# Batch 0's spectra made twice for one filter tile, tables issued by SP, and another order of the first loads

## The chip, the core and the metric

The kernel runs on one core of a Trainium2 chip. The metric is device time in microseconds of one execution. The kernel before took 525.09 us in the median of three runs (524.14 to 527.62). A core has five engines with a queue of instructions each: PE (TensorE, matrix products into PSUM), DVE (VectorE), ACT (ScalarE), POOL (GpSimd) and SP (SyncE, which only issues transfers here). POOL's transfers can turn float32 into float16 on the way; SP's only copy. Engines run side by side and wait for one another through semaphores.

## The reference

```python
def _attn_ref(x, filt_r, filt_i):             # x: 8 x 3136 x 256
    X = np.fft.rfft(x, axis=1)
    F = (filt_r + 1j * filt_i)[None, :, :]    # 1569 x 256
    return np.fft.irfft(X * F, n=x.shape[1], axis=1)

def _moe_ref(x, U, V, w_ch1, w_ch2):          # x: the result above
    xt = x.transpose(0, 2, 1)
    h = xt @ U @ V                            # rank 32, over the sequence
    u = x + h.transpose(0, 2, 1)
    ch = np.maximum(u @ w_ch1, 0.0) @ w_ch2   # 256 -> 1024 -> 256
    return u + ch
```

So each of 8 batches goes through a Fourier transform over 3136 positions, a product with a filter of one complex number per frequency and channel, the transform back, a low-rank mixing over the sequence, and a two-layer perceptron per position.

## The kernel before

**The transform.** 3136 is 64 x 49. A first matmul (with `w64`, 64 points) gives 32 slots `s`, each a complex part; a second one per slot (table `t2`, 98 x 128) does the 49 points and leaves, for one slot, the real parts of its spectrum on partitions 0 to 63 and the imaginary parts on 64 to 127. The product with the filter follows on DVE, then a matmul per slot with the inverse table (`g12`) and a last matmul with `s2`. The kernel calls the steps f1, forward, product, inverse. Slots are worked in 16 pairs `m`; tables and filters are cut in four `PARTS` of eight slots.

**The filter product.** `ft` has two halves in its columns: filt_r and filt_i. The first half is copied to partitions 64 to 127 (`swap_real`, L221), the second is copied there with its sign turned (`swap_imag`, L228). `both_products` (L521) reads one PSUM bank `px` twice, once against each half, in one DVE instruction of 1024 elements. The matching inverse table has two halves as well: `g`, and `g` with its upper and lower 64 rows exchanged. The second half of part 0 is loaded ready-made (`gs`, L247); those of parts 1 to 3 are made by two POOL copies each (`swap_table`, L186). Batches 0 and 1 use this form. From batch 2 on `product` (L531) uses three DVE instructions and a POOL addition.

**Batch 0** does not go through DRAM. `first_f1` (L356) makes the 64-point transform in groups of four rows for half the channels (`dh`), evicted by ACT and DVE in turn into `at`. `first_a` (L385) turns two slots into the layout of forward, evicted by ACT into `a`. `first_mid` (L399) then runs over m: the product of m on DVE, the inverse of m-1 on PE with two ACT evictions (`back`, L405), forward of m+2 (`ahead`, L421), `first_a` of m+3. Between sets of four pairs it makes the two filter copies of the next part. `keep_on` and `keep_in` (L342, L350) are matmuls whose result nobody reads. `fill` are 13 units of batch 1's f1 (`f1_units`, L457), four of them inside `first_mid`'s loop, four among its last transpositions, and the rest until the first perceptron group. At the end, seven groups of transpositions are evicted to `e2`, from which the low-rank part and the perceptron start.

**Batches 1 to 7** store f1's result to DRAM (`c1`, by SP for batch 1) and load it back as `a` (`load_a`, L493, on SP), likewise after the inverse (`c2`, `load_e`). Their steps are laid out by hand on `slots`: 48 slots per batch, two for every two hidden blocks of a group of four row pairs. `put(slot, gen)` names the slot at which a step's instructions are written into all queues; each engine then works its queue strictly in the written order. mm1 (L707), mm2 (L722) and the stores of `out` fill the slots themselves.

**The loads** stand at the start of POOL's queue, in this order: x of batch 0 in three chunks, called x(0,0), x(0,1), x(0,2) here, with single filter rows (`load_rest`) after the first and x's odd last row after the last; filters of part 0, tables `t2` and `g` of part 0, `gs`; then for each further part table t2, filters, table g, with the copies of `swap_table` a part later; x(1,0), U, x(1,1), x(1,2), V (`vq`), four pieces of `w1`, `w2` (as `w2n`), x(2,0); then 14 copies that reorder V (`v_order`, L277), x(2,1), and two copies that reorder w2. POOL lets eight transfers be under way: a ninth waits for the first.

**PSUM** has eight banks: tags x and f one each, m four, o two.

Of the kernel before, what the change touches and what calls it, by code (L numbers as in the profile page):

```python
# [26 lines left out]
def _consts():  # L27
# [22 lines left out]
    for s in range(NS):  # L50
        for j in range(49):
# [10 lines left out]
            if s:  # L62
                t2[s, :49, j], t2[s, 49:, j] = e.real, -e.imag
                t2[s, :49, 64 + j], t2[s, 49:, 64 + j] = sg * e.imag, sg * e.real
                g[s, j] = np.concatenate([ei.real, ei.imag]) * 2
                g[s, 64 + j] = np.concatenate([-ei.imag, ei.real]) * 2 * sg
            else:
                o = 0 if j < 25 else 49
                t2[s, o:o + 49, j] = e.real
                t2[s, o:o + 49, 64 + j] = e.imag  # L70
                g[s, j, o:o + 49] = ei.real * (2 if f else 1)
                g[s, 64 + j, o:o + 49] = -ei.imag * 2

    t2[0, :, 64] = 0
    t2[0, 49:, 64] = (-1.0) ** r
    g[0, 64] = 0
    g[0, 64, 49:] = (-1.0) ** r
    g *= ESC / n
    gs = np.concatenate([g[:, 64:], g[:, :64]], 1)
# [5 lines left out]
            np.ascontiguousarray(g.reshape(4, 8, 128, 98).transpose(0, 2, 1, 3)).astype(f16),  # L85
            np.ascontiguousarray(gs[0:8].transpose(1, 0, 2)).astype(f16))
# [3 lines left out]
def kernel(  # L90
# [13 lines left out]
    w64_np, s2_np, idn_np, fold_np, wp_np, t2_np, g_np, gs_np = _consts()  # L104
# [7 lines left out]
    gs_d = nc.inline_tensor(gs_np, name="gsd")  # L112
# [8 lines left out]
    BUFS = {"x": 1, "f": 1, "m": 4, "o": 2}  # L121

    def bank(tag, name):
        return ps.tile([128, 512], F32, tag=tag, bufs=BUFS[tag], name=name)

# [21 lines left out]
    def load_x(b, c, parts=None):  # L147
# [3 lines left out]
        for lo, hi in parts or ((c0[c], c0[c + 1]),):  # L151
            for h in range(2):
# [6 lines left out]
            if hi == NH:  # L159
# [3 lines left out]
                nc.gpsimd.dma_start(t[0:64, o:o + DM], rows(x, b, NR - 1, 1))  # L163
# [9 lines left out]
    nyq = sb.tile([128, DM], F32, tag="ocho", bufs=1, name="nyq")  # L173
    PARTS = ((0, 8), (8, 16), (16, 24), (24, 32))
    for a, b in PARTS:
        for c in (0, NS * DM):
            nc.vector.memset(ft[32:64, c + a * DM:c + b * DM], 0.0)  # L177

    def load_table(k, a, b):

        dst, src, w = ((t2, t2_d, 128), (g12, g_d, 98))[k]
        n, p = (b - a) * w, dst.shape[0]
        nc.gpsimd.dma_start(dst[:, a * w:b * w],
                            bass.AP(tensor=src, offset=a // 8 * p * n, ap=[[n, p], [1, n]]))

    def swap_table(a, b):  # L186

        o = NS * 98
        for p, q in ((0, 64), (64, 0)):
            nc.gpsimd.tensor_copy(g12[p:p + 64, o + a * 98:o + b * 98],  # L190
                                  g12[q:q + 64, a * 98:b * 98])

    def load_filters(a, b):

        d = max(a, 1)
        for c, src in ((0, filt_r), (NS * DM, filt_i)):
            nc.gpsimd.dma_start(
                ft[0:24, c + a * DM:c + b * DM],
                bass.AP(tensor=src.tensor, offset=a * DM, ap=[[64 * DM, 24], [1, (b - a) * DM]]))
            nc.gpsimd.dma_start(  # L200
                ft[25:49, c + d * DM:c + b * DM].rearrange("p (k d) -> p k d", d=DM),
# [3 lines left out]
    def load_rest():  # L205

        for c, src in ((0, filt_r), (NS * DM, filt_i)):
            nc.gpsimd.dma_start(
                ft[25:49, c:c + DM],
                bass.AP(tensor=src.tensor, offset=32 * DM, ap=[[64 * DM, 24], [1, DM]]))  # L210
            nc.gpsimd.dma_start(
                ft[24:25, c:c + NS * DM],
                bass.AP(tensor=src.tensor, offset=24 * 64 * DM,
                        ap=[[NS * DM, 1], [1, NS * DM]]))
        nc.sync.dma_start(
            nyq[64:65, :],
            bass.AP(tensor=filt_r.tensor, offset=(SEQ // 2) * DM, ap=[[DM, 1], [1, DM]]))

    def swap_real(a, b):

        nc.vector.tensor_copy(ft[64:128, a * DM:b * DM], ft[0:64, a * DM:b * DM])  # L221

    def swap_imag(a, b):

        fb = NS * DM
        if a == 0:
            nc.vector.memset(ft[0:1, fb:fb + DM], 0.0)
        nc.vector.tensor_scalar_mul(ft[64:128, fb + a * DM:fb + b * DM],  # L228
                                    ft[0:64, fb + a * DM:fb + b * DM], -1.0)
# [3 lines left out]
    for c in range(1, len(CH)):  # L233
        load_x(0, c)
# [4 lines left out]
    for k, part in enumerate(PARTS):  # L239
        if k:  # L240
            load_table(0, *part)
        load_filters(*part)
        if k == 0:
            load_table(0, *part)
        load_table(1, *part)
        if k == 0:
            nc.gpsimd.dma_start(g12[:, NS * 98:(NS + 8) * 98], gs_d.ap())  # L247
        if k > 1:
            swap_table(*PARTS[k - 1])
    load_x(1, 0)  # L250
    uq = sb.tile([128, NR * RANK], F16, tag="esb", bufs=2, name="uq")
    nc.vector.memset(uq[64:128, :], 0.0)
    nc.gpsimd.dma_start(uq[0:64, :], moe_U.rearrange("(q r) p -> q (r p)", q=NQ))
    load_x(1, 1)
    swap_table(*PARTS[3])
    load_x(1, 2)
    vqs = []
    for k in range(2):
        v = sb.tile([128, SEQ // 2], F16, tag="xt", bufs=5, name="vq")
        vqs.append(v)  # L260
        nc.gpsimd.dma_start(v[64:96, :], moe_V[:, k * (SEQ // 2):(k + 1) * (SEQ // 2)])
    w1 = cst.tile([128, 2 * 1024], F16)
    for i in range(4):
        nc.gpsimd.dma_start(
            w1[32 * i:32 * i + 32, :].rearrange("p (h c) -> p h c", h=2),
            bass.AP(tensor=moe_w_ch1.tensor, offset=moe_w_ch1.offset + i * 64 * 1024,
                    ap=[[1024, 32], [32 * 1024, 2], [1, 1024]]))
    w2 = cst.tile([128, 8 * DM], F16)
    w2n = sb.tile([128, 8 * DM], F16, tag="esb", bufs=2, name="w2n")
    nc.gpsimd.dma_start(w2n, moe_w_ch2.rearrange("(cc t) e -> cc (t e)", t=8))  # L270
# [6 lines left out]
    def v_order():  # L277

        for r in range(0, NR, 8):
# [8 lines left out]
            yield  # L288

# [60 lines left out]
    def keep_in(tile, n):  # L350

        for _ in range(n):
            nc.tensor.matmul(tile[:, 0:128], w64[:, :], idn[:, :],
                             start=True, stop=True, skip_group_check=True)

    def first_f1():  # L356
        ne = 0
        xs = [st[0]["x"][c] for c in range(len(CH))]
        for r0 in range(0, NH - 1, 4):
            for dh in range(2):  # L360
                keep_on(4 if r0 < 16 else 0)
# [6 lines left out]
                for h in range(2):  # L368
                    dst = atv[:, dh, :, h * NH + r0:h * NH + r0 + 4]
                    src = pa.rearrange("p (r h k) -> p h k r", h=2, k=64)[:, h]  # L370
                    if ne % 2:
                        nc.vector.tensor_copy(dst, src)
                    else:
                        nc.scalar.copy(dst, src)
                    ne += 1
        pa = bank("m", "pa")
        o = (NH - 1 - c0[-2]) * DM
        for dh in range(2):
            nc.tensor.matmul(pa[:, dh * 64:(dh + 1) * 64],
                             xs[-1][0:64, o + dh * 128:o + (dh + 1) * 128], w64[0:64, 0:64],  # L380
                             start=True, stop=True, skip_group_check=True)
        nc.scalar.copy(atv[:, :, :, NH - 1],
                       pa[:, 0:128].rearrange("p (e k) -> p e k", e=2))
# [13 lines left out]


    def first_mid(fill):  # L399
# [21 lines left out]
        def ahead(m, keep=0):  # L421
            return forward(m, st[0]["a"][m // 4], ("m",), keep)

        pxs = [ahead(0), ahead(1)]
        keep_on(8)
        for m in range(NS // 2):
            for k, part in enumerate(PARTS):
                if k and 2 * m == part[0]:
                    swap_real(*part)
                    swap_imag(*part)  # L430
# [509 lines left out]
```

## Time and profile before

| what | value |
|---|---|
| runs of before, median of 3 | 525.09 us (524.14 to 527.62) |
| the profiled execution: its time | 523.76 us |
| its span, first to last instruction | 522.0 us |
| DVE busy, ACT busy, POOL busy, of the span | 78%, 72%, 58% |
| first product of batch 0 starts | 19.98 us |
| first matmul of the perceptron (phh, L712) starts | 53.61 us |
| first forward of batch 1 (px, L516) starts | 64.45 us |
| HBM read, written | 56.25 MB, 48.17 MB |

All times in what follows are microseconds from the start of the span. "Busy" adds up the instructions of an engine. A row of the order in time gives start, length, engine, line, operation, result<-operands, and in brackets how long the engine had been idle and what ended that. A matmul's row includes the time until its result is in PSUM, so rows of PE overlap; the pitch from one start to the next is what a matmul costs in a series. Transfers issued by POOL have their landing on record, those issued by SP have not.

### The profile page before, as it was taken

To read this page: it belongs to the slowest core of one execution; us is meant where nothing else is said; L and a number is where in the kernel's file an instruction comes from. 1 tells how busy PE (TensorE), PEld (TensorE's weight loads), DVE (VectorE), ACT (ScalarE), POOL (GpSimd) and SP (SyncE) were. 2 spreads that over 40 slices of the span, in tenths; PEclk is the share of its full clock that TensorE was granted. 3 is DMA by queue.
4 is the path that set the end of the run, shared out by engine and by line. 5 is a ranking of instruction groups with operands and counts; after the bars stand their busy time and mean duration, and the time that the engine had idled before them with its cause. 6 is when DMAs were issued, how large, how long until landed. Compare 5 with 4: busy or idle time off the path is not lost.

```text
span 522.0 us, 11372 instructions
## 1 busy us (share of the span) xinstructions
PE 496.7 (95%) x3976; PEld 327.4 (63%) x3976; DVE 407.7 (78%) x585; ACT 377.5 (72%) x772; POOL 301.9 (58%) x430
## 2 busy tenths in 40 slices
PE   4878899999989999999999999999999999999997
PEld 3766477777656665666666666666666666555555
DVE  7897386677888888998998888988999877436654
ACT  2767757768778768887788878888777678665552
POOL 7798733445765757775777675965666564313001
PEclk9999999999999999999999999999999999999999
DMA  8989998978899798887898698888777575644325
GB/s 135 188 143 221 233 214 203 213 209 191 197 202 253 180 203 181 215 219 176 235 216 221 162 253 207 184 227 194 180 194 150 129 167 134 139 100 80 71 62 121
DMA packets 122571, 93.99 MB, mean 180 GB/s; under 512 B 58017, under 2 KB 104866, under 8 KB 122514
## 3 DMA queue, kind: packets, MB, share of 16 engines
q1 hardware_dynamic: 98986, 50.93, 39.1%
q0 software_dynamic: 20240, 40.60, 37.9%
q10 hardware_dynamic: 3288, 1.74, 1.3%
q8 instruction: 31, 0.51, 0.4%
q14 instruction: 26, 0.21, 0.1%
HBM read 56.25 MB, written 48.17 MB: 200 GB/s over the span
## 4 chain that ended last, share of the span: by engine, by line
PE 78%; DVE 9%; DMA 6%; POOL 3%; issue 2%; ACT 1%; ACTq 0%; SPq 0%; DVEq 0%; POOLq 0%
PE phh L712 28%; PE po L789 25%; PE px L516 5%; PE pi L552 5%; PE pu L637 4%; PE po L738 4%; DVE uv L537 4%; DMA xt<-in_x_dram 3%; PE pf L472 3%; PE ph L594 2%; DVE ft L177 1%; DVE uv L535 1%; DMA out_dram<-och 1%; DMA g<-gd 1%; DMA a<-c 1%
## 5 line engine op out<-in xcount | busy, mean ns | idle before, releaser
L720 ACT ACTIVATE h<-phh 128x512 f16<-128x512 f32 (+1 forms) x391 | 205.4, 578 | 68.6 <-PE phh L712 64.1
L712 PE MATMUL phh<-ut,w 128*128 128x512 f16 x768 | 197.5, 379 | 0.3 <-ACT h L720 0.3
L540 POOL TENSOR_TENSOR y<-uv 128x512 f16<-128x512 f16 x96 | 111.8, 1165 | 100.1 <-DVE uv L537 80.3
L789 PE MATMUL po<-h,w 128*128 128x512 f16 x656 | 168.5, 379 | 0.0
L712 PEld LDWEIGHTS <-w 128*128 128x128 f16 x832 | 114.2, 144 | 54.5 <-issue 0.9
L537 DVE TENSOR_TENSOR uv<-px,ft 64x512 f16<-64x512 f32 x192 | 132.1, 688 | 2.6
L807 POOL DMA_DIRECT2D out_dram<-och x148 | 85.9, 588 | 81.6 <-DVE och L799 38.9
L789 PEld LDWEIGHTS <-w 128*128 128x128 f16 x656 | 60.5, 98 | 57.8 <-issue 1.1
L535 DVE TENSOR_TENSOR uv<-px,ft 128x512 f16<-128x512 f32 x96 | 64.9, 676 | 35.2 <-PE px L516 33.0
L556 ACT CAST esb<-pi 98x512 f16<-98x512 f32 x112 | 65.9, 589 | 32.1 <-PE pi L552 28.2
L798 DVE TENSOR_TENSOR tt<-po,ut 128x512 f32<-128x512 f32 x82 | 56.7, 692 | 34.3 <-PE po L789 32.3
L799 DVE STREAM_TRANSPOSE och<-tt 128x512 f32<-128x512 f32 x82 | 58.4, 712 | 2.8
L516 PE MATMUL px<-a,t 98*128 98x256 f16 x256 | 49.1, 273 | 5.6 <-DVE uv L537 2.8
L478 ACT CAST asb<-pf 128x512 f16<-128x512 f32 (+1 forms) x80 | 46.1, 576 | 6.5 <-PE pf L472 3.8
L524 DVE TENSOR_TENSOR uv<-px,ft 128x1024 f16<-128x1024 f32 x32 | 38.0, 1219 | 11.7 <-PE px L516 11.2
L702 ACT CAST ut<-pu 128x512 f16<-128x512 f32 x82 | 44.8, 612 | 0.0
L516 PEld LDWEIGHTS <-t 98*128 98x128 f16 x256 | 22.7, 98 | 31.6 <-DVE uv L537 10.6
L552 PE MATMUL pi<-y,g 128*98 128x256 f16 x192 | 36.7, 272 | 0.1
L472 PE MATMUL pf<-xt,w 128*128 128x512 f16 (+1 forms) x91 | 33.2, 370 | 1.0 <-DMA xt<-in_x_dram 1.0
L738 PE MATMUL po<-w,h 128*128 128x256 f16 x256 | 33.2, 273 | 0.0
L552 PEld LDWEIGHTS <-g 128*98 128x98 f16 x256 | 29.6, 123 | 3.2 <-issue 0.8
L637 PEld LDWEIGHTS <-e 96*128 96x128 f16 x686 | 26.4, 98 | 7.2
(99 smaller groups left out, 420.0 us busy)
## 6 DMA issues: line engine op xcount, KB each, us to landing
xt<-in_x_dram POOLq DMA_DIRECT2D x46, 256.0 KB, 6.6
out_dram<-och SPq DMA_DIRECT2D x180, 64.0 KB
a<-c SPq DMA_DIRECT2D x28, 384.0 KB
e<-c SPq DMA_DIRECT2D x56, 192.0 KB
out_dram<-och POOLq DMA_DIRECT2D x148, 64.0 KB, 3.5
c<-esb SPq DMA_DIRECT2D x24, 384.0 KB
c<-asb POOLq DMA_DIRECT2D x30, 256.0 KB, 5.6
out_dram<-och POOLq DMA_DIRECT2D x12, 256.0 KB, 4.8
```

The costliest lines, as they stand in the source:

```text
L516: nc.tensor.matmul(px[:, sl * DM:(sl + 1) * DM], t2[:, s * 128:(s + 1) * 128], a2[:, (2 * ml + sl) * DM:(2 * ml + sl + 1) * DM], start=Tru ...
L535: nc.vector.tensor_mul(uv[:, 0:512], px[:, :], ft[:, a:a + 512])
L537: nc.vector.tensor_mul(uv[p:p + 64, 512:1024], px[q:q + 64, :], ft[q:q + 64, b:b + 512])
L540: nc.gpsimd.tensor_add(y, uv[:, 0:512], uv[:, 512:1024])
L552: nc.tensor.matmul(pi[0:98, sl * DM:(sl + 1) * DM], g12[:, g:g + 98], y[:, o:o + DM], start=(fi == 0), stop=(fi == nf - 1), skip_group_che ...
L556: nc.scalar.copy(split(esb[:, ml * 512:(ml + 1) * 512]), natural(pi[0:98, :]))
L712: nc.tensor.matmul(pm[:, 0:w], w1[:, dh * 1024:(dh + 1) * 1024].rearrange("p (c t) -> p t c", t=8)[:, t], ut[:, dh * w:(dh + 1) * w], star ...
L720: nc.scalar.activation(h[:, 0:w], pm[:, 0:w], RELU)
L789: nc.tensor.matmul(po[:, :], w2[:, t * DM + dh * 128:t * DM + (dh + 1) * 128], hs[gx, t][:, :], start=(t == 0), stop=(t == 7))
L798: nc.vector.tensor_add(tt, po[:, :], uts[gx][:, dh * 512:(dh + 1) * 512])
L799: nc.vector.transpose(och.rearrange("p (j h a) -> p h j a", h=2, a=32)[:, dh], tt.rearrange("p (j t) -> p j t", t=32))
L807: (nc.gpsimd if k and (b < nb - 1 or r0 > 12) else nc.sync).dma_start(dst, och[32 * i:32 * i + 32, k * 512:(k + 1) * 512] .rearrange("p (r ...
```

## The change

1. **One filter tile for batch 0.** filt_r is loaded to partitions 0 to 63 of `ft`, filt_i to 64 to 127. `ahead` makes a slot's real parts on both partition halves of one PSUM bank and its imaginary parts on both halves of a second one: eight matmuls with 64 columns of `t2` each, in pairs at column positions 0 and 64, instead of two with 128 columns. One DVE instruction multiplies both banks by the same 512 columns of `ft`. The copies between the sets of four are gone; the last frequency (f = 1568) becomes a row of its own in the tables, so the separate row `nyq` goes as well. `ft` is brought into the old form for the later batches by 16 DVE instructions (`spread_filters`), one at the end of `first_mid`, one after `make_u(0)`, 14 at slots 0, 1, 2, 3, 4, 5, 6, 8, 12, 17, 27, 30, 36, 44. Four of these turn a sign after batch 1.
2. **No negated table loaded.** `gs` goes. For each of the four parts POOL makes one copy (`swap_table`) and ACT one with the sign turned (`negate_table`, at m = 0, 4, 8, 12).
3. **Tables by SP.** `t2` and `g` are issued by SP. Ahead of each part stands a transfer of one element (`mark`) that reads an eviction of batch 0: that of row 12 in `first_f1` for part 0, that of `a`'s first piece of set 0, 1, 2 for parts 1, 2, 3; so SP holds the tables until then.
4. **POOL's order.** x's odd row stands ahead of x(0,2); filters of parts 0 and 1 follow, then swap 0, filters of parts 2 and 3, swap 1, U, x(1,0), swap 2, x(1,1), swap 3, x(1,2), V, w1, x(2,0), w2, eight of the 14 V copies, x(2,1), the w2 copies, the other six.
5. **PSUM** tag m lives in a pool of its own that is opened three times: for `first_f1`, for the two-bank `px` of `first_mid` (two buffers, so `ahead` of m+2 waits for the product of m), and for the rest.
6. **first_f1 and fillers.** ACT evicts one half of the channels, DVE the other. Fillers are laid out as 18, 4, 8, 4, 40, 3, 3, 3, 22, 0, 0, 0 between the groups; those inside `first_mid` go. One unit of `fill` stays in `first_mid`'s loop (m = 15), two follow it, five stand among the transpositions.
7. **Stores.** In batch 1, the first of eight stores of `out` goes from SP to POOL in five groups.

```diff
-            for c in (0, NS * DM):
-                nc.vector.memset(ft[32:64, c + a * DM:c + b * DM], 0.0)
+    for p in (32, 96):
+        nc.vector.memset(ft[p:p + 32, a * DM:b * DM], 0.0)
...
+    def spread_filters():
+        for a, b in PARTS:
+            lo, hi = slice(a * DM, b * DM), slice((NS + a) * DM, (NS + b) * DM)
+            for dst, src in ((ft[0:64, hi], ft[64:128, lo]), (ft[64:128, hi], ft[64:128, lo]),
+                             (ft[64:128, lo], ft[0:64, lo])):
+                nc.vector.tensor_copy(dst, src)
+                yield
+        for a, b in PARTS:
+            neg = ft[64:128, (NS + a) * DM:(NS + b) * DM]
+            nc.vector.tensor_scalar_mul(neg, neg, -1.0)
+            yield
...
+    def tables_behind(k, ap):
+        nc.sync.dma_start(mark[:, k:k + 1], ap)
+        for t in range(2):
+            load_table(t, *PARTS[k], eng=nc.sync)
...
+            if r0 == 12:
+                tables_behind(0, atv[0:1, 0, 0, r0:r0 + 1])
...
+        if ml == 0 and gi < 3:
+            tables_behind(gi + 1, st[0]["a"][gi][0:1, 0:1])
+            loads(gi + 1)
+            if gi == 2:
+                load_weights()
...
-        def ahead(m, keep=0):
-            return forward(m, st[0]["a"][m // 4], ("m",), keep)
+        def ahead(m):
+            px = pm[-1].tile([128, 1024], F32, tag="px", bufs=2, name="px")
+            for fi in range(2):
+                for sl in range(2):
+                    s, o = 2 * m + sl, fi * 512 + sl * DM
+                    for q in (0, 64):
+                        nc.tensor.matmul(
+                            px[q:q + 64, o:o + DM], t2[:, s * 128 + fi * 64:s * 128 + fi * 64 + 64],
+                            st[0]["a"][m // 4][:, s % KG * DM:(s % KG + 1) * DM],
+                            start=True, stop=True, tile_position=(0, q), skip_group_check=True)
+            return px
...
-            for k, part in enumerate(PARTS):
-                if k and 2 * m == part[0]:
-                    swap_real(*part)
-                    swap_imag(*part)
-            uv = both_products(m, pxs.pop(0))
+                nc.vector.tensor_mul(
+                    uv.rearrange("p (f e) -> p f e", f=2),
+                    pxs.pop(0).rearrange("p (f e) -> p f e", f=2),
+                    bass.AP(tensor=fap.tensor, offset=fap.offset, ap=[fap.ap[0], [0, 2], [1, 512]]))
...
+                if m % 4 == 0:
+                    negate_table(*PARTS[m // 4])
...
-                (nc.gpsimd if k and (b < nb - 1 or r0 > 12) else nc.sync).dma_start(
+                (nc.gpsimd if k and (b < nb - 1 or r0 > 12) or b == 1 and n == 0 and r0 < 20 else nc.sync).dma_start(
...
+    for t in (0, 1, 2, 3, 4, 5, 6, 8, 12, 17, 27, 30, 36, 44):
+        put(t, spread)
```

## The prediction

> **What bounds the kernel now.** I read the page first (who is busy), then a table of stretches, then the order in time of each engine over the first 65 us, which hold nearly all of the diff. Page, busy time:
>
> ```profile
> PE 496.7 (95%) x3976; PEld 327.4 (63%) x3976; DVE 407.7 (78%) x585; ACT 377.5 (72%) x772; POOL 301.9 (58%) x430
> ```
>
> Table of stretches (columns: stretch, its length, then PE, PEld, DVE, ACT, POOL busy, granted clock, DMA share, GB/s):
>
> ```profile
> 18.00:44.20 26.20, 21.81 (x328) 18.77 (x330) 25.51 (x26) 18.08 (x49) 23.29 (x35) 1.00 0.93 161
> 44.20:53.60 9.40, 8.44 (x108) 5.48 (x107) 6.33 (x13) 6.70 (x13) 8.37 (x13) 1.00 1.08 222
> 64.40:522.00 457.60, 447.88 (x3411) 289.71 (x3411) 359.70 (x521) 336.08 (x677) 249.18 (x343) 1.00 0.76 180
> ```
>
> From 64.4 us on PE is busy 98% and the diff touches little there. Between 18 and 44 us batch 0's products run, and DVE is busy 25.5 of 26.2 us: DVE sets that stage. What PE and DVE save before 64 us moves the whole rest, if the loads keep up; so the question is how much sooner batch 0 is done. Order in time, DVE:
>
> ```profile
> 18.88 0.69 DVE L228 TENSOR_SCALAR ft<-ft 64x2048 f16<-64x2048 f16 x1
> 19.98 4.62 DVE L524 TENSOR_TENSOR uv<-px,ft 128x1024 f16<-128x1024 f32 x4
> 24.63 0.69 DVE L221 COPY ft<-ft 64x2048 f16<-64x2048 f16 x1
> 25.24 1.32 DVE L228 TENSOR_SCALAR ft<-ft 64x2048 f16<-64x2048 f16 x1
> 26.67 4.62 DVE L524 TENSOR_TENSOR uv<-px,ft 128x1024 f16<-128x1024 f32 x4
> ```
>
> Four products take 4.62 us (1.155 each); between two sets of four stand two filter copies, about 2.05 us. The stage runs from 19.98 to 44.17 (fourth set: 39.55 + 4.61). POOL, same view, shows what feeds it:
>
> ```profile
> 12.17 0.59 POOL L183 DMA_DIRECT2D t<-t2d  x1 [0.61 <-DMA xt<-in_x_dram]
> 14.91 0.55 POOL L247 DMA_DIRECT2D g<-gsd  x1 [0.71 <-DMA xt<-in_x_dram]
> 25.05 2.22 POOL L190 COPY g<-g 64x784 f16<-64x784 f16 x2 [0.69 <-DMA g<-gd]
> 32.79 1.32 POOL L154 DMA_DIRECT2D xt<-in_x_dram  x2
> ```
>
> POOL issues wait for landed DMAs, so these waits date the landings: x(0,1) by 12.1, x(0,2) by 14.9, table g's second part 5.3 us after its issue at 19.70. PE, same view, shows what a matmul of half the columns costs:
>
> ```profile
> 70.45 0.39 PE L646 MATMUL pu<-s,e 128*128 128x128 f16 x4
> 70.78 0.39 PE L652 MATMUL pu<-low,hz 32*128 32x512 f16 x1
> 71.09 0.40 PE L646 MATMUL pu<-s,e 128*128 128x128 f16 x4
> 115.51 1.59 PE L594 MATMUL ph<-e,ul 64*32 64x256 f16 x49
> 117.03 0.44 PE L712 MATMUL phh<-ut,w 128*128 128x512 f16 x1
> ```
>
> 49 matmuls of 256 columns, each on 32 output rows, need 1.52 us: 0.031 each, where 256 columns alone take 0.109 (L552: 4 in 0.44). Four of different output rows run side by side.
>
> **Up to the first product.** x lands as before, with the 32 KB odd row ahead of the last 512 KB: by the 1.3 us between the last two landings (13.6, 14.9) for 256 KB, that is 0.16 us; so 15.1. Four groups at 0.22 follow, evicted in pairs (0.43 per ACT instruction): done near 17.3, before 17.98. Then transposition back 0.4, eviction 0.58, first spectra 0.7: 19.1. The two filter copies, the small memset and the nyq copy that stood at 17.9 to 19.9 are gone. The table is the second condition. Its part 0 left POOL's queue at 12.17; now SP issues it behind the eviction of rows 12, about 13.5, plus a marker DMA: at 14.2 to 14.5. SP loads of this kind show 4.7 us (a, 392 KB issued at 59.70, used at 64.45), which gives 19.2, and 19.8 for the first product; 2.0 (idn, a small one) is the other end. The fillers ahead of x(0,1) may delay rows 12: 40 of them are 4.3 us at the 0.107 each that matmuls of 128 columns take at 12 to 15 us, 2.2 at the 0.056 of 25 us (the granted clock reads 1.00 in both stretches); they start near 9.0 and x comes at 12.1, so 0 to 1.2 us. PE now works without a gap from 3.3 us, where before it paused from 9.2 to 12.0 and was fast only from 18 on, so I take 0, and 19.4: **-0.6** (ends -0.9 and +1.4).
>
> The Trainium skill, TensorE: Matmul & The Clock Gate, Part 1, has the array at half rate until about 3.4 us of sustained work are done. By that rule PE would be fast near 7 to 10 us and the delay 0; by the row, slow to 15 us, the sum would be 1.2 worse.
>
> DVE's eight memsets stay; the eviction of every other group on DVE waits for them until 10.4, and x is later.
>
> **The product stage.** Per pair of slots:
> - DVE: the same 1024 elements out of PSUM, 1.155. That these are now different elements in two banks instead of one bank read twice is not shown; equal count, equal time. Filter copies: none.
> - PE: inverse 8 x 0.043 = 0.35; transposition 4 x 0.055 = 0.22; spectra 8 instead of 2, as four side-by-side pairs 4 x 0.109 = 0.44. Going from full to part of the array and back costs 0.1 each time: L646 to L652 takes 0.33 where four of 0.056 are 0.22, and the way back 0.31 for 0.21. Sum 1.20; the fillers of before (4 or 14 per step) go.
> - ACT: eviction 0.49 plus two of 0.275 = 1.04, plus a negation of 64x784 every fourth step. No row has it: ACT's 128x512 takes 0.59 and 128x1024 takes 1.01, between them 0.75; 0.72 spread over four is 0.18. Sum 1.22.
>
> ACT is next in line: 13 steps of 1.22 and 3 of 1.155 = 19.3, against 24.2. Later tables: part 1 is issued behind the first eviction (18.4 + about 0.9), needed at first product + 3.5, with about 0.5 to spare; parts 2 and 3 likewise leave 4.5 us or so. At 4.7 us that is 0.2 each; I take 0.5 (ends 0 and 6.3, from the 6.6 us of x's loads). POOL: second half of a table is one copy (0.9) instead of two, four times instead of three (6.5 us before, 3.6 to 4.2 now); nine table DMAs leave (9 x 0.58 = 5.2). The next filters stand behind swap 0, the last swaps behind the tables: filters for step 8 issue by 22.6 and land by 28, needed at 28.6. x(1,0) is issued near 25.5 instead of 32.8. SP has nothing behind its markers until the c writes at 44.8. Stage: 19.8 instead of 24.2, **-4.4**.
>
> **Behind it.** Units of the next batch's first transform move from the stage (four) to behind it (one stays): three evictions more on DVE/ACT, in the 2.3 us in which DVE waited for the last inverse. 2.8 us of work into 2.3, one on ACT: **+0.3**. Sixteen filter copies (0.69 each, 11 us; 1.32 beside a POOL copy) now lie between 46 and 110 us. DVE is busy 38.5 of the 60 us from 50 to 110, so they fit, but one stands ahead of the last c evictions; c's write, its landing and a's load (59.70 + 4.7) hang on these, and PE already waits for a: **+0.6** (0 to 0.9). The rest, near 105 us where DVE is late: **+0.3** (0 to 0.7).
>
> x(2,0) goes ahead of w2 (512 KB). PE waits for x here 0.71 and 0.27 us; its load, issued at 46.3 and used at 57.7, queued behind w2: **-1.0** (0 to -1.0). w2 and its POOL copies then end near 53, first use 63 less the gain. The five stores: 0.58 each on POOL (13 of 20 us busy), ahead of products' sums that have two steps in hand; 0.46 less each on SP, ahead of a's loads: 0, ends -0.5 and +0.3.
>
> Sum: -0.6 - 4.4 + 0.3 + 0.6 + 0.3 - 1.0 = **-4.8**. The profiled execution is 523.76 (span 522.0, 1.76 around it), so 519.0 there; it lies 1.33 below the median of 525.09. On the median: **520.3**.
>
> **Rivals.**
> 1. All margins hold: products at DVE's 1.155 (18.5, -5.7), first product at 19.1 (-0.9), no wait for a: with -1.0 and +0.3, -7.3, so 517.8. For: ACT's excess is 0.07 a step and negation could fall into slack. Against: three engines within 0.07 us.
> 2. The loads give the gain back. DMA share is 1.08 from 44.2 to 53.6 and 0.93 in the stage: idle there about 1.8 us of 26.2, plus 0.75 for the table no longer loaded: only 2.5 us can move forward: 522.6. Against: x(2,0) no longer behind w2.
> 3. Slower: the tables come late. They are issued 2 us later than now, not sooner, while the queues carry x and filters. Each of four parts that lands L after issue holds the products by L - 4.1 (part 0) or L - 4.5. Break-even is 4L - 17.6 = 4.8 + 0.7, L = 5.8; POOL-issued tables show 5.0 to 5.7 in median, x 6.6. At 7.5: +11.7, so 532.0. Against: 4.7 for double the bytes on SP.
> 4. Pairs not side by side: 8 x 0.109, PE 1.64 a step, 16 x 0.42 = 6.7: 527.0. Against: the row of 49, where four with the same 64 input rows share 0.109.
>
> The Trainium skill, TensorE: Matmul & The Clock Gate, Part 3, says that weight loads overlap running matmuls only across row groups; a pair here shares its rows, so by that rule loads stand free and rival 4's time comes about. The row of 49 speaks against it.
>
> **How the numbers follow.** Forecast 0.44, rival 1 0.28, rival 2 0.12, rival 3 0.10, rival 4 0.06. About 1% (5.25 us) is what a measurement here can tell from no change. Faster by more: rival 1 and a third of the forecast, 0.42. Slower by more: rival 3 and a tail of 4, 0.12. Within: 0.46. Range 516.5 to 524.5: from rival 1 less the stores' 0.5 and 0.8 of spread (the three runs of before reach 0.95 below their median) to rival 2 with tables landing after 5.0 us (4 x 5.0 - 17.6 - 0.7 = +1.7); it leaves out 3 and 4 and a little at the ends. The forecast's own: 518.5 to 522.5.
>
> **What would show it.** First product at 19.4; sixteen products without copies between them, 1.2 us apart, ending near 39.2; pairs starting together; no PE wait for x(2,0) near 53; a longer one for a near 59.5. Wrong if DVE waits for spectra whose PE waits for table DMAs, or if PE idles for x or w2 between 45 and 60.

## The result, and the profile after

The changed kernel takes 529.52 us in the median of 13 runs (526.21 to 532.88), the kernel before 524.40 beside it (13 runs, 521.91 to 527.62): a ratio of 1.0091, 95% interval 1.0062 to 1.0120. It is slower by 0.9%, where a gain of 0.9% was forecast. Its profiled execution is 529.52 as well, with a span of 527.7; the one of before is 523.76 with 522.0. Three runs of the experiments below, two of e14 (530.4 and 530.5) and one of e12 (533.0), lie more than 1.5% above the fastest of their kernel and are left out of the intervals there, but not of the medians.

Where the loss lies is read from the same five events in both traces:

| start of | before | after | difference |
|---|---|---|---|
| first product of batch 0 | 19.98 | 20.59 | +0.61 |
| 16th product | 42.95 | 45.17 | +2.22 |
| first phh | 53.61 | 56.36 | +2.75 |
| first px of batch 1 | 64.45 | 69.63 | +5.18 |
| last phh | 516.00 | 521.43 | +5.43 |

So it arises in two places: before the 16th product, where 4.4 were to be gained, and between the first phh and batch 1's first px. Behind that the distance changes little.

The table of stretches of after (columns as in the prediction): the first 7.5 us of the products, the rest of them, and everything from batch 1's px on.

```profile
20.60:28.10 7.50, 7.13 (x68) 4.85 (x67) 4.93 (x5) 4.09 (x9) 7.50 (x13) 0.54 0.79 124
28.10:46.40 18.30, 14.84 (x233) 11.22 (x232) 14.67 (x13) 14.21 (x39) 7.88 (x15) 1.00 0.80 150
69.60:527.70 458.10, 448.39 (x3411) 289.70 (x3411) 365.14 (x527) 336.17 (x677) 252.98 (x348) 1.00 0.77 180
```

DVE no longer sets the stage (14.7 busy of 18.3). In the first stretch PE's granted clock is 0.54. The last row is that of before (447.88 of 457.60), as the prediction had it. The order in time of DVE in the product stage:

```profile
20.59 2.59 DVE L470 TENSOR_TENSOR uv<-px,ft 128x1024 f16<-128x1024 f32 x2 [3.68 <-PE px L456]
23.54 1.23 DVE L470 TENSOR_TENSOR uv<-px,ft 128x1024 f16<-128x1024 f32 x1 [0.36 <-PE px L456]
26.28 1.22 DVE L470 TENSOR_TENSOR uv<-px,ft 128x1024 f16<-128x1024 f32 x1 [1.51 <-PE px L456]
28.07 3.69 DVE L470 TENSOR_TENSOR uv<-px,ft 128x1024 f16<-128x1024 f32 x3 [0.56 <-DMA ft<-in_filt_r_dram]
33.01 4.94 DVE L470 TENSOR_TENSOR uv<-px,ft 128x1024 f16<-128x1024 f32 x4 [1.25 <-PE px L456]
39.20 4.93 DVE L470 TENSOR_TENSOR uv<-px,ft 128x1024 f16<-128x1024 f32 x4 [1.25 <-PE px L456]
```

The copies between the sets are gone, and within a set the pitch is 1.24. But there is a gap in each later set of four (1.25 ahead of 33.01 and of 39.20, 1.03 ahead of the last product), and the first four products take 7.48 (20.59 to 28.07) where four at 1.24 are 4.95. The row at 28.07 names a load of filters, but the filters of this part were in by 21.02 by POOL's landings, and the product starts 0.05 behind the end of its spectra (28.02, the row of PE at 27.36 below), as the others do: it waits for PE. PE's waits between 14 and 75 us (total, times, longest) name the causes:

```profile
PE pi L441 <- ACT g L199: 3.6, 4, 1.1
PE px L563 <- DMA a<-c: 2.4, 1, 2.4
PE px L456 <- DMA t<-t2d: 2.0, 1, 2.0
PE pf L520 <- DVE h L765: 1.1, 1, 1.1
```

First line: PE waits for ACT's negated table, about 1.1 three times. Third: for table t's part 0, which SP issues at 14.34 and PE uses at 19.87. What the third did to the clock is seen in PE's order in time:

```profile
17.40 0.50 PE L372 MATMUL keep<-idn,w 128*128 128x128 f16 x6
19.87 0.63 PE L456 MATMUL px<-a,t 98*64 98x256 f16 x8 [1.97 <-DMA t<-t2d]
21.84 0.66 PE L418 MATMUL pt<-idn,at 128*98 128x128 f16 x4
22.43 1.06 PE L456 MATMUL px<-a,t 98*64 98x256 f16 x8
27.36 0.66 PE L456 MATMUL px<-a,t 98*64 98x256 f16 x8
29.55 0.39 PE L418 MATMUL pt<-idn,at 128*98 128x128 f16 x4
29.86 0.63 PE L456 MATMUL px<-a,t 98*64 98x256 f16 x8
```

The same eight matmuls step 1.00 after the wait (22.43 to 23.43) and 0.57 later (29.86 to 30.43). POOL's order in time shows what its copies of table g hold up:

```profile
20.55 0.83 POOL L194 COPY g<-g 64x784 f16<-64x784 f16 x1 [4.67 <-DMA g<-gd]
27.31 1.19 POOL L157 DMA_DIRECT2D xt<-in_x_dram  x2
34.20 0.84 POOL L194 COPY g<-g 64x784 f16<-64x784 f16 x1 [5.71 <-DMA g<-gd]
40.83 0.84 POOL L194 COPY g<-g 64x784 f16<-64x784 f16 x1 [4.68 <-DMA g<-gd]
49.19 1.17 POOL L157 DMA_DIRECT2D xt<-in_x_dram  x2 [2.49 <-PE pf L520]
50.44 0.58 POOL L308 DMA_DIRECT2D w2n<-in_moe_w_ch_dram  x1
60.34 2.47 POOL L313 COPY w<-w2n 128x1024 f16<-128x1024 f16 x2 [2.16 <-DMA w2n<-in_moe_w_ch_dram]
```

x(1,0) goes out at 27.31, but then the queue stands for 5.7 and 4.7 us. w2, issued at 45.72 before, is issued at 50.44 here. The DMA share from 40 to 50 us is 0.77; it was 1.10. Last, DVE behind the first phh:

```profile
57.50 0.69 DVE L524 CAST asb<-pf 128x512 f16<-128x512 f32 x1
58.22 3.70 DVE L230 COPY ft<-ft 64x2048 f16<-64x2048 f16 x4
61.96 0.69 DVE L765 TENSOR_SCALAR h<-phh 128x512 f16<-128x512 f32 x1
```

Four spread copies in a row stand ahead of the first h. Three take 0.69 each; the fourth takes 1.58, beside POOL's copies of w2 (60.34).

### The profile page after: what moved, and what is told of

It is laid out like the page before. It is cut to its first block, busy times and chain, and to the rows that moved or that the text cites. A ratio compares the mean times of both kernels' runs of the same rounds, so it can differ in the third digit from the quotient of the medians.

```text
span 527.7 us, 11543 instructions
## 1 busy us (share of the span) xinstructions
PE 502.2 (95%) x4055; PEld 328.9 (62%) x4055; DVE 417.7 (79%) x594; ACT 378.2 (72%) x773; POOL 298.6 (57%) x424
## 4 chain that ended last, share of the span: by engine, by line
PE 75%; DVE 6%; POOL 2%; issue 2%; ACT 1%; DMA 1%; ACTq 0%; DVEq 0%; POOLq 0%; SPq 0%
PE phh L759 28%; PE po L836 25%; PE pi L599 5%; PE px L563 5%; PE pu L684 4%; PE po L785 4%; DVE uv L584 4%; PE pf L520 3%; PE ph L641 2%; DVE uv L582 1%; POOL out_dram L854 1%; POOL y L587 1%; DMA a<-c 1%; PE pu L699 0%; DVE uv L571 0%
## 5 line engine op out<-in xcount | busy, mean ns | idle before, releaser
L854 POOL DMA_DIRECT2D out_dram<-och x153 | 88.8, 588 | 80.8 <-DVE och L846 39.7
L563 PE MATMUL px<-a,t 98*128 98x256 f16 x224 | 43.1, 273 | 6.9 <-DVE uv L584 3.3
L526 ACT CAST asb<-pf 128x512 f16<-128x512 f32 (+1 forms) x77 | 44.3, 575 | 7.5 <-PE pf L520 4.9
L563 PEld LDWEIGHTS <-t 98*128 98x128 f16 x224 | 19.8, 98 | 32.3 <-DVE uv L584 11.7
L157 POOL DMA_DIRECT2D xt<-in_x_dram x50 | 30.0, 607 | 3.4 <-PE pf L520 2.5
```

The costliest lines, as they stand in the source:

```text
L563: nc.tensor.matmul(px[:, sl * DM:(sl + 1) * DM], t2[:, s * 128:(s + 1) * 128], a2[:, (2 * ml + sl) * DM:(2 * ml + sl + 1) * DM], start=Tru ...
L854: (nc.gpsimd if k and (b < nb - 1 or r0 > 12) or b == 1 and n == 0 and r0 < 20 else nc.sync).dma_start(dst, och[32 * i:32 * i + 32, k * 51 ...
```

## The experiments

Theories, one for each place: W, the wait for table t lowers PE's clock; N, the negations are waits of their own; G, POOL's waits for table g leave the load queues idle; C and V, the spread copies hold c and h; X and Q, it is the new place of w2 or of x(2,1); rivals L (tables late whatever else), A (a's own transfers) and M (the copies cost the same anywhere). The expectations use a few more letters: F in e1 (filters or tables pace the products anyway), H and Q in e4 (the hold made the table late; the queues are shared and full), B in e6 and e7 (what A says). All runs in one table; e1 to e3 have 4 runs each, e16 has 6, the others 9 to 13; the intervals are of the ratio to before; "way" is from the first phh to batch 1's px, in the profiled execution. Before lies between 524.1 and 524.6 in every set of runs.

| run | us | ratio, 95% interval | products, first to 16th | first phh | way |
|---|---|---|---|---|---|
| before | 524.40 | 1 | 22.97 | 53.61 | 10.84 |
| after | 529.52 | 1.0062 to 1.0120 | 24.58 | 56.36 | 13.27 |
| e1_warm | 529.06 | 1.0068 to 1.0153 | 22.39 | 54.53 | 12.81 |
| e2_negpool | 531.30 | 1.0101 to 1.0153 | 24.32 | 56.08 | 13.81 |
| e3_warm_negpool | 530.94 | 1.0095 to 1.0143 | 23.06 | 55.48 | 15.44 |
| e4_t0_early | 526.60 | 1.0042 to 1.0115 | 21.78 | 53.24 | 13.27 |
| e5_loads_first | 528.27 | 1.0054 to 1.0111 | 23.92 | 54.86 | 13.80 |
| e6_tables_neg_early | 524.33 | 0.9969 to 1.0024 | 19.17 | 50.64 | 12.86 |
| e7_all_early | 526.68 | 1.0011 to 1.0067 | 22.04 | 53.66 | 13.11 |
| e8_spread_late | 527.29 | 1.0034 to 1.0082 | 22.14 | 52.93 | 13.40 |
| e9_w2_first | 525.19 | 0.9984 to 1.0036 | 19.17 | 50.09 | 13.64 |
| e10_x21_late | 526.76 | 1.0010 to 1.0074 | 20.01 | 50.40 | 14.92 |
| e11_old_order | 526.58 | 1.0007 to 1.0072 | 19.17 | 51.33 | 14.38 |
| e12_old_order_spread_late | 525.98 | 0.9991 to 1.0049 | 20.02 | 50.79 | 15.11 |
| e13_w2_paced | 525.14 | 1.0006 to 1.0054 | 19.17 | 50.22 | 12.20 |
| e14_x21_late_paced | 523.41 | 0.9948 to 1.0000 | 20.02 | 51.78 | 10.70 |
| e15_e6_paced | 526.45 | 1.0022 to 1.0070 | 20.02 | 51.02 | 13.51 |
| e16_after_paced | 532.78 | 1.0121 to 1.0198 | 24.63 | 55.88 | 12.96 |
| e17_paced_in_gaps | 523.23 | 0.9942 to 0.9997 | 20.67 | 52.20 | 11.11 |
| e18_before_x20_first | 524.16 | 0.9954 to 1.0008 | 22.68 | 54.64 | 11.22 |

**The clock (W) and the negation on another engine.** e1: fillers through the wait. e2: POOL turns the sign. e3: both.

```diff
-            keep_on(6)
+            keep_on(50)                  # e1, e3
             pxs = [ahead(0)]
-        nc.scalar.mul(g12[64:128, ...], g12[0:64, ...], -1.0)
+        nc.gpsimd.tensor_scalar_mul(g12[64:128, ...], g12[0:64, ...], -1.0)   # e2, e3: right behind swap_table
```

> One number changes: 50 filler matmuls instead of 6 ahead of the first spectra of batch 0, so that PE works on while it waits for the first table (17.9 to 19.9 us in the changed kernel). Theory W (the pause makes PE fall to half rate, granted clock 0.5 from 20.6 to 27.5 us, and this spaces the first four products 1.4 to 2.7 us apart): granted clock stays 1.00, products 0 to 4 lie 1.24 apart, product 4 starts 2.5 to 3 us sooner, the sixteenth ends near 43.5 instead of 46.4, time 3 to 4 us below that of the changed kernel, near 526. Rival F (the filters' landing or the tables pace the first products anyway): product 4 moves by less than 1 us, time within 1 us of 529.5.

> The four sign-turned copies of the inverse table go from ACT (written just ahead of their use) to POOL, directly behind the other copy. Theory N (PE waits 1.07 us for ACT's negation at pairs 4, 8, 12 and 0.37 at 0, and DVE with it): the three waits of PE on ACT's table line vanish, no pause of 1.25 us of DVE ahead of products 7, 11, 15, the sixteenth product ends 3.0 to 4.0 us sooner. POOL gives x of batch 1 out 0.9 to 3.4 us later. Rival L (the table itself lands so late that the wait only changes its name): PE waits for POOL instead, for 0.5 to 1.5 us each, and the end moves by less than 1 us. The clock may still fall in this kernel.

> Both edits together. If W and N are the two losses of the product stage and are independent, the gains add: sixteenth product ends near 40 (6 to 7 us sooner than 46.4), first perceptron matmul near 50, time near 523 to 524, so just below the kernel before. If tables and filters are the real pace, the second edit gives less than half of what it gave alone.

The stretch table of e1 for the first products:

```profile
20.60:28.10 7.50, 6.72 (x104) 4.88 (x102) 6.55 (x6) 5.30 (x13) 7.50 (x13) 1.00 0.84 132
```

With work in the wait the clock stays at 1.00 and the stage is 2.2 us shorter: W holds. The time hardly moves. At px of batch 1 e1 is 2.3 us ahead of the changed kernel, but there the clock falls instead (PE waits 2.8 for a, then half clock from 68.6 to 72.0), and at phh 24 (counted from 0) it is ahead by 1.2. In e2 POOL's tensor_scalar takes 2.17 to 2.19 a part, ACT's 0.85; PE's wait only changes its name (for POOL's g, 3.6 in two waits). e2 and e3 are therefore no clean test of N.

**The table earlier.** e4 sets the mark of part 0 behind rows 4 instead of rows 12.

```diff
-            if r0 == 12:
+            if r0 == 4:
                 tables_behind(0, atv[0:1, 0, 0, r0:r0 + 1])
```

> SP holds table part 0 only until row group 4 is evicted (near 8.5 us) instead of group 12 (13.5). Theory H (the hold made the table late): the wait of 1.97 us for table t goes, first product near 19.3 instead of 20.6, PE does not pause and stays at full rate, time 3 to 5 us below the changed kernel. Rival Q (the transfers share one saturated set of queues, DMA share 1.06 in 10 to 20 us): x's last rows land as much later as the table lands sooner (1.5 to 2 us), and the first product stays at 20 to 21.

The table is issued at 9.72, PE waits 0.4 for it (and 0.7 for x ahead of that), the clock stays full through the stage, products 0 to 4 are 1.13 apart. 2.9 us of the loss are gone in the median; three waits for ACT's negation (3.2 in all) and a way of 13.3 remain.

**The negation and the later parts (N), and POOL's loads (G).** e6: every part is issued one mark earlier, and the negation of parts 1 to 3 is written two products before its first use. e5: x(1,1) and x(1,2) ahead of the third part's copy, the fourth part's copy behind V and w1, on top of e4. e7: both.

```diff
-                if m % 4 == 0:
-                    negate_table(*PARTS[m // 4])
+                if m == 0 or m % 4 == 2 and m < 12:
+                    negate_table(*PARTS[(m + 2) // 4])
```

> Each part of the tables is issued one mark earlier, and ScalarE writes the negation of parts 1 to 3 two products before its first use. Theory N (each part's negation is a serial wait of TensorE: 1.07 us three times, since ScalarE writes it right before the product that reads it): the three waits PE<-ACT go, products 4 to 15 are 1.24 apart throughout, the stage from product 4 to 15 takes 13.6 instead of 17.1 us, the first phh is near 50 and the time 521 to 523 if nothing behind it gives the gain back. Rival L (the tables land late whatever ScalarE does): the waits change their name to SP's table t or GpSimd's table g, the first phh stays at 52 to 53.5. Rival B (all that is gained before the first phh is waited for again at batch 1's a, whose loads and stores take as long as before): the first phh near 50, but px of batch 1 still at 65 or later, time 525 or more.

> The run with table t's part 0 earlier, and on GpSimd the loads x(1,1) and x(1,2) issued ahead of the wait for table g's third part, the fourth part's copies behind the loads of V and w1. That run had the first phh at 53.2 and px of batch 1 at 66.5, 13.3 apart (10.8 in the kernel before). Theory G (GpSimd's waits for table g, 2.3 and 5.0 us there, leave the load queues idle in the product stage, so that w2, x(2,0) and x(2,1) run into batch 1's c and a): the waits for g stay, but x(1,2) is issued about 7 us earlier, x(2,0) and w2 leave the queues some 2 us earlier, the first phh stays within 0.5 of 53.2 and px of batch 1 comes 1.5 to 2.5 us earlier, 64 to 65; time about 524.5. Rival C (the distance of 13.3 comes from the spread copies in VectorE's queue, which hold the last c): px of batch 1 stays at 66 to 67 and the time at 526.6.

> The two edits together (tables and negations earlier, x(1,1) and x(1,2) ahead of the third table part's wait). If N and G both hold: first phh near 50, px of batch 1 at 61 to 63, time 519 to 522, faster than the kernel before. If one of them fails the run equals the other edit alone. If rival B holds (batch 1's a is bound by its own transfers), px of batch 1 is at 65 or later and the time 524 to 527.

PE's longest waits in e6:

```profile
PE px L564 <- DMA a<-c: 2.2, 1, 2.2
PE px L457 <- DVE uv L471: 1.2, 1, 1.2
PE px L457 <- ACT a L420: 1.0, 3, 0.3
PE pu L694 <- DVE h L766: 0.9, 1, 0.9
```

No wait for ACT's g among them: N holds, and L falls, for no wait for a table has come instead. The products need 19.17, 3.8 less than in the kernel before. Of e1 to e8 this is the only one that brings the time down to that of before (0.9996). But of the 3.0 us gained at the first phh, 0.9 are left at px of batch 1. e5 shows that G fails: with x(1,1) and x(1,2) issued early the DMA share is 1.12 from 30 to 40 and 0.36 from 40 to 50, since x(2,0) waits for a buffer that batch 1's f1 must free (7.0 us in e5, 6.3 in e7); nothing comes earlier, and in e5 PE waits 1.5 for a later part of table t besides. In e7 the late fourth copy costs PE 2.0 and a stretch at half clock.

**The way to batch 1's px: load orders (X, Q) and first copies (C).** e8 is e4 with the two first spread copies two slots later. e9 to e12 stand on e6: e9 w2 ahead of x(2,0); e10 x(2,1) and w2's copies behind all of V's; e11 both; e12 both and e8's edit.

```diff
-        load_x(2, 0)                                  # e9, e11, e12
         w2n = sb.tile([128, 8 * DM], F16, tag="esb", bufs=2, name="w2n")
         nc.gpsimd.dma_start(w2n, moe_w_ch2.rearrange("(cc t) e -> cc (t e)", t=8))
+        load_x(2, 0)
...
-            if k == 3:                                # e10, e11, e12: after the loop
-                load_x(2, 1)
```

> The run with table t's part 0 earlier, and the two spread copies of V that lay ahead of batch 1's last c moved two slots later. Rival C (VectorE's and GpSimd's copies hold the last c): batch 1's last c is issued 0.8 to 1.2 us earlier behind the first phh (3.1 there), a follows by as much and px of batch 1 is near 65.5, time about 525.6. Theory G (the queues are full in that window): c is issued earlier, but lands no earlier, px of batch 1 stays at 66 to 67 and the time at 526.6.

> The run with tables and negations earlier (524.3 against 524.6 of the kernel before; first phh 50.6, batch 1's last c issued 53.75, a issued 59.40, px of batch 1 at 63.5 behind a wait of 2.25 for a), and w2 loaded ahead of x(2,0) as in the kernel before. There x(2,0) waits for a buffer until 43.5 and w2 is issued behind it at 44.7, while the load queues stand idle from 42 to 45. Theory X (the exchange of x(2,0) and w2 holds w2 back, and its 512 KB then run beside batch 1's c): w2 is issued near 38.5 and landed before 48, GpSimd's wait of 2.3 for it goes, c's last write lands 0.5 to 1 us sooner, px of batch 1 at 62.5 to 63. Rival Q (it is x(2,1), issued at 51.2 ahead of the last c): w2 earlier, but c takes 5.65 us as before and px of batch 1 stays at 63.5.

> The run with tables and negations earlier, and x(2,1) with the copies of w2 behind all of V's copies, as in the kernel before. Theory Q (x(2,1), 512 KB, issued at 51.2 ahead of batch 1's last c at 53.75, makes that c's landing take 5.65 us where it took 4.0 in the kernel before): x(2,1) is issued near 55, c lands in 4.0 to 4.5, a is issued near 58 and px of batch 1 comes at 62 to 62.3, time about 523. Rival X (w2, still issued at 44.7, is what fills the queues): no change, px of batch 1 at 63.5.

> Both orders as in the kernel before: w2 ahead of x(2,0), and x(2,1) behind V's copies. If the orders of GpSimd's loads are what lengthens the way from the first phh to px of batch 1 (10.8 in the kernel before, 12.9 here): it goes back to 10.8 to 11.3, px of batch 1 at 61.5 to 62 and the time at 521.5 to 522.5, faster than the kernel before by 0.4 to 0.6%. If the rest is VectorE's spread copies in front of the evictions: it stays at 12.0 or more.

> The same with the first two spread copies two slots later. If VectorE's copies still hold batch 1's last c (issued 3.1 behind the first phh, 2.1 in the kernel before): c 0.5 to 1 us earlier, px of batch 1 as much, time 521 to 522. If not: as the run with the old order, within 0.3.

In e8 the last c goes out 2.28 behind the first phh instead of 3.10 in e4, but a follows it by 7.1 us instead of 6.1: C alone falls. Each load order does what it was blamed for, and the way is no shorter. In e9 PE no longer waits for a; in e10 and e11 a is issued 3.4 and 2.0 us behind the last c, where e6 needs 5.65. Instead PE waits for h (2.8, 2.2, 2.1), with a half clock of 3.4 us behind that wait in each, and, where x(2,1) is late, for x(2,1) (1.7, 1.4). In e12 the last c goes out 2.55 behind the first phh, 3.40 in e11, but PE waits 1.7 for h and 2.1 for x(2,1), each with a half clock behind it, and the way is 15.11. DVE in e9:

```profile
51.84 4.71 DVE L230 COPY ft<-ft 64x2048 f16<-64x2048 f16 x4
56.58 0.69 DVE L766 TENSOR_SCALAR h<-phh 128x512 f16<-128x512 f32 x1
```

and PE:

```profile
57.33 0.59 PE L694 MATMUL pu<-s,e 128*128 128x128 f16 x4 [2.75 <-DVE h L766]
```

The four copies in a row take 4.71 beside POOL's copies of w2 and V, 2.76 alone. So no single load order is the cause, and X and Q alone fall.

**Pacing the copies (V against A and M).** No spread copy ahead of slot 4, four by slot 8 (the expectations miscounted: they say six, or five), the rest one by one among batch 1's products: e13 on e9, e14 on e11 (batch 2's units from the fifth on one slot later), e15 on e6, e16 on the changed kernel itself.

```diff
-    for t in (0, 1, 2, 3, 4, 5, 6, 8, 12, 17, 27, 30, 36, 44):
+    for t in (4, 5, 6, 8, 10, 12, 14, 15, 17, 19, 20, 22, 27, 30, 36, 44):
         put(t, spread)
```

> The run with tables and negations earlier and w2 ahead of x(2,0) (525.2; first phh 50.1, px of batch 1 at 63.7), with VectorE's spread copies paced: none ahead of slot 4, six by slot 8 instead of eleven, the rest one by one through batch 1's products. There four spread copies in a row (4.71, alone they would take 2.76: they run beside GpSimd's copies) stood ahead of the first h, and TensorE waited 2.75 for it. Theory V (the spread copies, which the kernel before makes inside its product stage, are what holds the way from the first phh to px of batch 1): the wait for h goes, px of batch 1 comes at 61.5 to 62.7, bounded by a issued near 58.5, and the time is 523 to 524. Rival A (a's transfers set px of batch 1 whatever VectorE does): TensorE waits for a instead, px of batch 1 at 63 to 64, time 525. Rival M (the copies cost as much wherever they stand): px of batch 1 earlier, but six copies of 0.7 come back between 64 and 90, time 525.

> The run with both load orders of the kernel before (526.6; a issued 56.7, two us earlier than elsewhere, but TensorE waits 2.1 for h and 1.4 for x(2,1), px of batch 1 at 65.7), with the spread copies paced and batch 2's units from its second chunk on one slot later. Theory V: without these two waits and the half clock behind them px of batch 1 comes at 60.5 to 61.5 and the time is 522 to 523. Rival A: TensorE waits for a up to 63 or later, time 525.

> The run with tables and negations earlier (524.3; px of batch 1 at 63.5 behind waits of 0.93 for h and 2.25 for a), with the spread copies paced. Theory V: batch 1's last c 0.6 to 1 us earlier behind the first phh, no wait for h, px of batch 1 at 62.3 to 62.8, time 523 to 523.6. Rival A: only the wait for a grows, px of batch 1 at 63.5, time 524.3. Rival M: time 525.

> The changed kernel with nothing but the spread copies paced. Theory V: batch 1's last c is issued 2.1 to 2.5 behind the first phh instead of 3.1, the wait of 1.15 for h goes, px of batch 1 near 68.3 instead of 69.6 and the time about 528.2. Rival A: 529.5, px of batch 1 at 69.6. Rival M: 530 or more.

The wait for h is gone in all four, and in e14 the way is 10.70, that of the kernel before. So V holds for the way, but only with the load orders put back (what the later units of batch 2 add in e14 was not run apart): in e13, e15 and e16 PE waits 2.6 to 2.9 for a instead (A, where the orders are wrong). And M holds behind it. Between phh 24 and 54 (68 to 95 us) e13 falls back from 2.03 ahead of the kernel before to 0.02 behind, e14 from 1.97 ahead to 0.22 behind; without pacing e6 and e9 keep their distance there to 0.01. PE's waits of e14 from 50 to 92 us, and the stretch from 64 to 92 of before and of e14:

```profile
PE px L562 <- DVE uv L570: 2.2, 5, 1.3
PE px L562 <- DMA a<-c: 1.3, 1, 1.3
```

```profile
64.00:92.00 28.00, 26.48 (x204) 20.24 (x202) 20.55 (x22) 17.05 (x33) 10.22 (x20) 1.00 0.92 211
```

```profile
64.00:92.00 28.00, 25.75 (x196) 19.66 (x196) 25.60 (x30) 16.98 (x33) 9.58 (x16) 1.00 0.88 208
```

DVE goes from 20.6 to 25.6 busy of 28: there is hardly a free place for the copies there. e16 shows that pacing alone does not help the changed kernel (1.0121 to 1.0198).

**What is left, and one order by itself.** e17 is e14 with eight copies ahead of batch 1's first product instead of four, two of them in DVE's idle time before the first h. e18 is the kernel before with w2 issued behind x(2,0).

```diff
-    for t in (4, 5, 6, 8, 10, 12, 14, 15, 17, 19, 20, 22, 27, 30, 36, 44):
+    for t in (1, 2, 4, 5, 6, 7, 8, 8, 13, 16, 19, 21, 27, 30, 36, 44):
```

> The run with both load orders of the kernel before, paced copies and batch 2's units a slot later (523.4, ratio 0.9974 [0.9948, 1.0000]; px of batch 1 10.7 us behind the first phh, but 1.8 us lost between 68 and 92, where TensorE waits 2.6 for VectorE's uv behind the copies), with eight instead of five copies ahead of batch 1's first product, two of them in VectorE's idle 2.1 us before the first h. Theory M' (what is lost there is the copies' own 0.7 each in a stretch in which VectorE is full): px of batch 1 stays 10.7 to 11.2 behind the first phh, the waits for uv fall to about 1.6, 0.8 to 1.2 us come back, time 522.2 to 523. If the copies in front of h delay it again: px of batch 1 11.5 or more behind the first phh, time 523.4 or more.

> The kernel before with one part of the change alone: x(2,0) ahead of w2 on GpSimd. By the prediction's term: TensorE's wait of 0.71 for x(2,0) at 57.7 goes, and with it up to 1.0 us, time 523.2 to 523.8. By theory X (in the changed kernel the exchange hurts only because x(2,0) first waits about 5 us there for a buffer, which holds w2 behind it): here x(2,0) finds its buffer free at 46, so w2 is issued 1.2 later at most and lands by 56, px of batch 1 moves by less than 0.7 either way, time 523.5 to 524.8.

e17 is the fastest version found: 0.9969, interval 0.9942 to 0.9997, against 1.0062 to 1.0120 of the change as it was made. It is the best of 18 versions and only just apart from the kernel before, and the profiled executions do not show it ahead (last phh at 516.03, before 516.00). PE's waits for uv of L570 from 68 to 140 us fall from 2.0 to 0.3, where the expectation had 1.6, but the time stays above the 522.2 to 523 expected. It still falls back by 2.2 against the kernel before between phh 24 and 102: 0.5 of this every run built on the change shows, 1.2 is one wait for ACT's esb, whose cause was not tested. In e18 PE's two waits for x (1.0) are gone, and a wait of 1.7 for a has come (a issued 5.1 behind the last c instead of 4.0); the way is 11.22 instead of 10.84. So the trace shows no gain of 1.0 by the exchange itself; the times (0.9954 to 1.0008) show no difference either, but are too wide to rule one out.

## Why the prediction was wrong, point by point

- **Up to the first product: -0.6, measured +0.61**, inside the ends given there. The rows of batch 0 were done as reckoned or sooner (PE's last group at 14.77; the 40 fillers took 2.40). The term that failed is the landing: 4.7, taken from a's rows at 60 us; measured 5.53 for table t (14.34 to 19.87), 5.8 for table g's part 0, 7.2 for a later part (27.00 to 34.20), and 9.7 in e4, where g's first part is issued at 10.13 beside x.
- **"I take 0" for the clock.** True up to 20.6. What was missing is what the table's lateness does: PE paused for 1.97 and got a half clock for 6.8 us. With 0.37 for the first negation this makes the first four products 7.48 instead of 4.95: +2.5. e1 and e4 show it from both sides. The Trainium skill, TensorE: Matmul & The Clock Gate, Part 1, has the clock halved after an idle window of about 3.4 us, the windows running freely. The traces agree on the step (but for the one at the very end, every half clock lasts 3.41 or 6.83 us) and on the free run (those of e3 start at 31.12, 61.84 and 72.08, whole multiples of 3.41 apart). But no window was all idle: pauses of 1.1 (e17) to 3.0 us (e5) were enough here, and not always: 2.25 in e6, 2.42 in after and 2.6 in e13 left the clock full. How a pause lies in the windows seems to matter: counted back from each half clock, PE was idle for 1.2 to 3.0 us of the 3.41 ahead of it, and after's 2.42 fell on two windows, with 1.22 and 1.65 idle. These numbers give no sharp limit (1.73 in one window of e10 left the clock full).
- **The pair: 1.20 on PE, 1.22 on ACT, 19.3 for 16.** Right: 1.237, by PE, and 16 of them are 19.8. Pairs run side by side (eight matmuls in 0.57), so rival 4 falls.
- **The negation: 0.18 a step.** With the late table this is the step that failed hardest. The amount was nearly right (0.85 a part, 0.72 assumed), but ACT writes it between the product and the inverse that reads it, so it is no work spread over four steps but a wait: three gaps of about 1.2, +3.5. Stage: 19.8 + 2.5 + 3.5 = 25.8 (20.59 to 46.40), not 19.8.
- **Behind the stage: +0.3.** Measured +0.5 (from the end of the 16th product to the first phh 9.44 before, 9.96 after).
- **Copies and the wait for a: +0.6 (0 to 0.9); x(2,0) ahead of w2: -1.0.** Together -0.4; measured +2.43. PE's waits for x(2,0) did go, but in e18 that brought nothing that can be seen: what x(2,0) gains is lost again at a. The copies were reckoned by busy time from 50 to 110 us, in which they fit; in the order of the queue four of them stand ahead of one h, and one takes up to 1.58 beside POOL's copies.
- **Near 105 us: +0.3; stores: 0.** Right: 5.18 becomes 5.43 at the end, and no place shows the stores.
- **Rival 3** gave the direction. But its mechanism (each late part holds the products) happened for part 0 alone; parts 1 to 3 were held by the negation and not by their landing (POOL had copied parts 2 and 3 of table g 2.0 and 1.5 us before ACT began to negate them). Rival 1 fell with the margins. Rival 2 was not run as such; in e6, where there is a gain to give back, 2.0 of 3.0 us are lost before px of batch 1.

In sum, the gain itself was real: tables and negation in time make the products 3.8 us shorter. About 2 us of it return with the spread copies in e13 and e14, and most of the rest with batch 1's c and a; with more of the copies in DVE's idle time (e17) 0.5 return between phh 24 and 54, but the wait for esb comes. 0.3% is the most that was kept. A last part of the result stays open: over the 13 runs the time follows the share of the span at a lowered clock (525.7 us plus 0.84 us per lost microsecond, 4.4 lost in the mean, correlation 0.94), so by this line, an estimate, some 1.3 us against before remain with a full clock, and how these divide between waits was not told apart.

## What to carry to other kernels

A step that is cheap by its busy time can still be a wait: look at which instruction it is queued behind and which one reads it next, and give it two steps of lead. Work taken out of a stage that an engine bounds is only saved if it is not done again on the same engine in front of the next critical result. And a pause of PE costs twice where the clock falls behind it, so time what a late table does to the clock, not only to the first matmul.

## What the runs showed of the hardware that was not expected

- POOL's tensor_scalar of 64x784 takes 2.17 to 2.19 us, its copy of the same shape 0.84; ACT's activation takes 0.85.
- DVE's copy of 64x2048 takes 0.69 alone and up to 1.58 beside POOL's copies, and POOL's copies of V grow from 0.72 to as much as 1.22. The Trainium skill, SBUF — State Buffer, "SBUF: two separate sides", has the two engines exclude each other on a shared pair of ports for a whole instruction. The rows are near it: 0.69 and 0.72 are 1.41, and beside the copies of V and w2 four of DVE's take 1.05 to 1.43 in e9.
- From the issue of a transfer by SP to the instruction that waits for it, it is 2.0 us (c in e11) to 9.7 us (table g in e4, beside x's loads).
